# Two attention blocks on one core: pipeline lag 4 to 0, B's PV product in head pairs, and warmup transposes in the tail

## The chip, the cores and the metric

The kernel runs on one core of one Trainium2 chip. The metric is the device time of one execution in microseconds (us). Times quoted are medians. A ratio is the mean time of one kernel's fast runs over the mean of the fast runs of the kernel before from the same rounds, so it is not quite the ratio of the medians beside it.

Engines are named as the profile names them: PE is TensorE (PEld its weight loads), ACT is ScalarE, DVE is VectorE, SP issues the transfers.

## The reference

There are two attention blocks, A and B, over cached keys and values, concatenated at the end. B has its own K and V for each of 32 heads; in A, 8 query heads share one of 4 K/V heads. Everything is bf16, and x is 16 batches of 32 query rows.

```python
# A: Hkv = 4 (repeated 8 times), B: 32 K/V heads; Sk = 1024, Dh = 128, D = 1024
q = (x @ wq).reshape(B, Sq, H, Dh).transpose(0, 2, 1, 3)
scores = einsum("bhqd,bhkd->bhqk", q, k) * Dh ** -0.5
o = einsum("bhqk,bhkd->bhqd", softmax(scores), v)
out = o.transpose(0, 2, 1, 3).reshape(B, Sq, H * Dh) @ wo
# result: concatenate([A's out, B's out], axis=-1)
```

## The kernel before

The work is cut into 128 units of B and 128 of A. A unit is four heads of one batch, so 4 x 32 = 128 query rows. One loop iteration takes one unit of B and one of A through scores, maximum, exponential, transpose of the probabilities, PV, norm and transpose of the output. It also transposes the keys of the next unit and does about one projection group of 8 matmuls. A ran four iterations behind B. This is the loop, cut:

```python
A_LAG = 4
for i in range(-1, last_it + 1):          # last_it = NU + A_LAG + 2, NU = 128
    ia = i - A_LAG
    sc("B", i)                            # scores: 8 matmuls, 32 weight columns x 512
    ot_evac("A", ia - 2, "act")           # ACT: A's transposed output to SBUF
    maxop("B", i)                         # DVE
    pv("B", i - 1)
    norm("B", i - 1)                      # DVE
    sc("A", ia); maxop("A", ia)
    expop("B", i)                         # ACT
    kt_B(i + 1, 0); kt_B(i + 1, 1)        # 16 transposes of keys, copied out by ACT
    proj(i, 0)                            # a projection group: 8 matmuls x 512
    recip("B", i); expop("A", ia)
    kt_B(i + 1, 2); kt_B(i + 1, 3)
    ...
    ot("B", i - 1); ot_evac("B", i - 1, "dve")
    pt("B", i); pt_evac("B", i)           # 8 transposes of the probabilities
    if (ia + 1) % 2 == 0:
        kt_A((ia + 1) // 2)               # every second iteration: A's keys
    pv("A", ia - 1); recip("A", ia); norm("A", ia - 1)
    ...
    pt("A", ia); pt_evac("A", ia)
    ot("A", ia - 1)                       # 1 transpose, reads what norm wrote
    # then the loads of the next units on SP
```

And this is B's PV. Each head has 32 query rows, so its weights (the transposed probabilities) fill only 32 of the array's 128 columns. Four heads sit beside each other, each with its own V:

```python
for c in range(KC):                       # 8 chunks of 128 keys
    for hh in range(4):
        e.matmul(PS[32*hh:32*hh+32, O_BANK, 0:DH], PTs[P][:, c, 32*hh:32*hh+32],
                 VB[u % NVB][:, hh, c, :], start=(c == 0), stop=(c == KC - 1),
                 tile_position=(0, 32 * hh))
```

## Time and profile before

| | before |
|---|---|
| time, median | 991.3 us (4 runs, 990.7 to 993.0) |
| PE busy | 926 of 991 us |
| first scores of B; second; last | 25.4; 33.0; 949.6 us |
| iteration, mean of numbers 5 to 119 | 7.23 us |
| iteration with / without A's key transposes (median) | 7.49 / 6.97 us |
| after the last scores of B | 41.4 us |

An iteration is read from the timeline as the distance between two starts of B's scores. Every second iteration also transposes A's keys. Those are the ones called "even" in the prediction (they are the odd-numbered ones in the code); the ones without are called "odd" there. I write "with keys" and "without keys" below. (The prediction's 7.53 and 7.01 us are single iterations; the medians are a little shorter.)

From the page of the kernel before: span, busy times, transfers, the chain that ended last by engine, and the group of B's PV.

```profile
span 991.0 us, 34534 instructions
PE 926.1 (93%) x15168; PEld 648.7 (65%) x15168; DVE 629.5 (64%) x1456; ACT 656.8 (66%) x1305; POOL 5.2 (1%) x14
DMA packets 172852, 341.96 MB, mean 345 GB/s; under 512 B 7328, under 2 KB 7328, under 8 KB 172704
PE 81%; DVE 8%; ACT 7%; issue 3%; DMA 1%; SPq 0%; POOL 0%; DVEq 0%; ACTq 0%
...
L576 PE MATMUL PS<-VB,PT_B 128*32 128x128 bf16 x4096 | 80.6, 220 | 0.4 <-ACT QO_A L626 0.4
```

PE carries 81% of the chain. The page's busy time cannot say how long PV occupies PE, because its matmuls overlap: 4096 matmuls of 220 ns each would be 901 us, and the union shows 80.6. The distance from one group's first start to the next group's first start says it. These are lines of the timeline of the kernel before (start us, length us, engine, line, operation, tiles, count, idle time before it).

```profile
506.97 0.62 PE L493 MATMUL PS<-KTB,QO_B 128*32 128x512 bf16 x8
507.50 0.48 PEld L576 LDWEIGHTS PS<-VB,PT_B 128*32 128x32 bf16 x32 [0.41 <-issue]
507.53 0.63 PE L576 MATMUL PS<-VB,PT_B 128*32 128x128 bf16 x32
507.92 0.18 PEld L493 LDWEIGHTS PS<-KTA,QO_A 128*32 128x32 bf16 x8
507.97 0.62 PE L493 MATMUL PS<-KTA,QO_A 128*32 128x512 bf16 x8
508.52 0.90 PEld L452 LDWEIGHTS PS<-ident,KB 128*128 128x128 bf16 x16 [0.42 <-issue]
```

PV starts at 507.53 and A's scores at 507.97: PV holds PE for 0.44 us. It streams 32 x 128 = 4096 columns in that time. One stream moves 128 columns in about 56 ns (16 key transposes in 0.90 us), so four must run side by side. The weights of A's scores are loaded ahead: their first load (507.92) precedes their first matmul.

Two waits of PE recur. In an iteration with keys, PE waits for ACT to empty a bank before A's key transposes; in every iteration it waits for DVE's norm before A's output transpose. Same kernel, timeline:

```profile
504.56 1.09 ACT L456 COPY KTB<-PS 128x512 uint32<-128x512 uint32 x2
504.57 0.61 PE L552 MATMUL PS<-ident,P_B 128*128 128x128 bf16 x8
505.31 0.61 PE L468 MATMUL PS<-ident,KA 128*128 128x128 bf16 x8
506.20 0.61 PE L552 MATMUL PS<-ident,P_A 128*128 128x128 bf16 x8
506.40 0.35 DVE L601 TENSOR_SCALAR O_A<-PS,rinv_A 128x128 bf16<-128x128 f32 x1 [0.42 <-PE PS L588]
506.81 0.23 PE L612 MATMUL PS<-ident,O_A 128*128 128x128 bf16 x1
```

Eight transposes take 0.45 us from start to start where nothing waits. The key transposes begin 0.74 us after the group before them (0.29 us waiting), and the output transpose 0.61 us after its predecessor (0.16 us; 0.33 us in the next iteration, without keys).

### The profile page before, as it was taken

What the parts mean: (1) busy time and instruction counts of PE and PEld (TensorE: products, weight loads), DVE (VectorE), ACT (ScalarE), POOL (GpSimd) and SP (SyncE); (2) the same over time, 40 slices, a digit from 0 to 9 for tenths busy, and PEclk for the clock granted to TensorE, in tenths of its full rate; (3) what the DMA queues carried; (4) which work ended last, traced back from release to release, by engine and by line L of the source; (5) the groups of instructions that cost most, each with busy time, mean ns of one, the idle gap of its engine ahead of it and who ended that gap; (6) DMA issues with size and microseconds to landing.
All of it is one profiled execution on the core that took longest, in us unless ns stands there. A gap on an engine that the chain in (4) does not pass through costs nothing.

```text
span 991.0 us, 34534 instructions
## 1 busy us (share of the span) xinstructions
PE 926.1 (93%) x15168; PEld 648.7 (65%) x15168; DVE 629.5 (64%) x1456; ACT 656.8 (66%) x1305; POOL 5.2 (1%) x14
## 2 busy tenths in 40 slices
PE   6899899899999999999999999999999999989985
PEld 3566667666676666667666666766666676666652
DVE  0346666666566666666677666776667777776762
ACT  2667677676676767777666776667676666766641
POOL 0000000000000000000000000000000000000000
PEclk9999999999999999999999999999999999999996
DMA  9998999999999999999999999999999999999800
GB/s 339 387 347 291 388 386 342 329 386 386 378 363 372 366 370 343 386 344 386 361 356 373 355 381 343 383 361 363 372 345 385 343 388 358 369 389 339 302 26 21
DMA packets 172852, 341.96 MB, mean 345 GB/s; under 512 B 7328, under 2 KB 7328, under 8 KB 172704
## 3 DMA queue, kind: packets, MB, share of 16 engines
q1 hardware_dynamic: 172064, 337.67, 94.0%
q8 instruction: 119, 1.95, 0.8%
q0 software_dynamic: 640, 2.10, 0.5%
q14 instruction: 29, 0.24, 0.1%
HBM read 337.64 MB, written 2.10 MB: 343 GB/s over the span
## 4 chain that ended last, share of the span: by engine, by line
PE 81%; DVE 8%; ACT 7%; issue 3%; DMA 1%; SPq 0%; POOL 0%; DVEq 0%; ACTq 0%
PE PS L452 22%; PE PS L493 12%; PE PS L368 11%; PE PS L345 11%; PE PS L552 8%; PE PS L576 6%; DVE PT_B L562 4%; PE PS L468 4%; PE PS L612 3%; PE PS L588 3%; ACT KTB L456 2%; ACT P_B L524 2%; DVE O_A L601 2%; ACT P_A L524 1%; DMA W_Q<-in_B_wq_dram 1%
## 5 line engine op out<-in xcount | busy, mean ns | idle before, releaser
L452 PEld LDWEIGHTS PS<-ident,KB 128*128 128x128 bf16 x4096 | 238.4, 98 | 98.4 <-issue 52.2
L452 PE MATMUL PS<-ident,KB 128*128 128x128 bf16 x4096 | 272.8, 219 | 14.8 <-ACT KTB L456 14.5
L456 ACT COPY KTB<-PS 128x512 uint32<-128x512 uint32 x512 | 275.3, 599 | 1.0 <-PE PS L452 0.9
L524 ACT ACTIVATE P_B<-PS,nmx_B 128x1024 bf16<-128x1024 f32 x128 | 142.5, 1113 | 199.3 <-DVE P_B L513 199.3
L513 DVE TENSOR_SCALAR_CACHE_REDUCE P_B<-PS 128x1024 bf16<-128x1024 f32 x128 | 156.7, 1224 | 55.6 <-PE PS L493 49.7
L513 DVE TENSOR_SCALAR_CACHE_REDUCE P_A<-PS 128x1024 bf16<-128x1024 f32 x128 | 155.5, 1215 | 2.8 <-PE PS L493 2.7
L524 ACT ACTIVATE P_A<-PS,nmx_A 128x1024 bf16<-128x1024 f32 x128 | 145.4, 1136 | 10.2 <-DVE P_A L513 10.2
L629 DVE COPY QO_B<-PS 128x128 bf16<-128x128 bf16 x128 | 28.7, 224 | 164.4 <-PE PS L612 164.4
L562 DVE COPY PT_B<-PS 128x512 uint32<-128x512 uint32 x128 | 88.5, 692 | 31.7 <-PE PS L552 31.7
L562 DVE COPY PT_A<-PS 128x512 uint32<-128x512 uint32 x128 | 88.5, 692 | 12.3 <-PE PS L552 6.5
L576 PEld LDWEIGHTS PS<-VB,PT_B 128*32 128x32 bf16 x4096 | 62.4, 96 | 46.6 <-issue 45.5
L626 ACT COPY QO_A<-PS 128x128 bf16<-128x128 bf16 x128 | 34.0, 265 | 74.4 <-PE PS L612 74.4
L493 PE MATMUL PS<-KTA,QO_A 128*32 128x512 bf16 x1024 | 79.6, 381 | 2.1 <-DVE PT_A L562 2.1
L552 PE MATMUL PS<-ident,P_A 128*128 128x128 bf16 x1024 | 78.5, 220 | 2.8 <-ACT P_A L524 2.8
L576 PE MATMUL PS<-VB,PT_B 128*32 128x128 bf16 x4096 | 80.6, 220 | 0.4 <-ACT QO_A L626 0.4
L588 PE MATMUL PS<-VA,PT_A 128*128 128x128 bf16 x1024 | 79.1, 220 | 1.9 <-DVE QO_B L629 1.2
L493 PE MATMUL PS<-KTB,QO_B 128*32 128x512 bf16 x1024 | 78.8, 384 | 0.7 <-ACT KTB L456 0.7
L552 PE MATMUL PS<-ident,P_B 128*128 128x128 bf16 x1024 | 78.1, 219 | 0.7 <-ACT P_B L524 0.7
L552 PEld LDWEIGHTS PS<-ident,P_A 128*128 128x128 bf16 x1024 | 62.9, 98 | 4.3 <-ACT P_A L524 3.3
L345 PE MATMUL PS<-xT_B,W_Q 128*128 128x512 bf16 x256 | 62.8, 392 | 2.6 <-DMA W_Q<-in_B_wq_dram 2.6
L588 PEld LDWEIGHTS PS<-VA,PT_A 128*128 128x128 bf16 x1024 | 60.4, 98 | 5.7 <-DVE QO_B L629 1.4
L552 PEld LDWEIGHTS PS<-ident,P_B 128*128 128x128 bf16 x1024 | 62.5, 98 | 0.9 <-ACT P_B L524 0.9
(50 smaller groups left out, 817.6 us busy)
## 6 DMA issues: line engine op xcount, KB each, us to landing
KB<-in_B_k_cache_dram SPq DMA_DIRECT2D x128, 1024.0 KB, 7.6
VB<-in_B_v_cache_dram SPq DMA_DIRECT2D x128, 1024.0 KB, 8.5
KA<-in_A_k_cache_dram SPq DMA_DIRECT2D x64, 256.0 KB, 7.8
VA<-in_A_v_cache_dram SPq DMA_DIRECT2D x64, 256.0 KB, 7.9
W_Q<-in_B_wq_dram SPq DMA_DIRECT2D x16, 512.0 KB, 8.9
W_O<-in_B_wo_dram SPq DMA_DIRECT2D x16, 512.0 KB, 8.5
W_Q<-in_A_wq_dram SPq DMA_DIRECT2D x12, 512.0 KB, 9.1
W_O<-in_A_wo_dram SPq DMA_DIRECT2D x8, 512.0 KB, 8.3
```

What stands on the lines that cost most here:

```text
L345: last = e.matmul(PS[:, pbank, 0:T], W[slot][:, c, j * DH:(j + 1) * DH], xT[P][:, c, :], start=(c == 0), stop=(c == DC - 1))
L368: last = e.matmul(PS[:, pbank, :], QO[P][s][:, j, 4 * tg:4 * tg + 4, :].rearrange("p b q -> p (b q)"), W[slot][:, j, nh * 512:(nh + 1) * 5 ...
L452: last = e.transpose(psbf(bk)[:, c * 128:(c + 1) * 128], KB[u % NKB][:, hh, c, :], ident[:])
L456: plan.use("act", lambda e: e.copy(KTB[hs][:].bitcast(U32), PS[:, bk, :].bitcast(U32)), writes=[r_KTB[hs]], banks=[bank[bk]], name="ktev_B ...
L468: last = e.transpose(psbf(bk)[:, c * 128:(c + 1) * 128], KA[m % NKA][:, c, :], ident[:])
L493: last = e.matmul(PS[32 * hh:32 * hh + 32, sbk + half, :], QO[P][s][:, 4 * jh + hh, b, :], kts[hh][:, half * 512:(half + 1) * 512], start= ...
L513: plan.use("dve", lambda e: e.tensor_scalar(Psb[P][:], PS[:, sbk:sbk + 2, :], -scale, None, ALU.mult, ALU.min, accum_out=nmx[P][:, k:k + 1 ...
L524: plan.use("act", lambda e: e.activation(Psb[P][:], PS[:, sbk:sbk + 2, :], AF.Exp, bias=nmx[P][:, k:k + 1], scale=scale, accum_out=rsum[P] ...
L552: last = e.transpose(psbf(bk)[:, c * 128:(c + 1) * 128], src, ident[:])
L562: plan.use("dve", lambda e: e.tensor_copy(PTs[P][:].rearrange("p c n -> p (c n)").bitcast(U32), PS[:, bk, :].bitcast(U32)), writes=[r_PT[P ...
L576: last = e.matmul(PS[32 * hh:32 * hh + 32, O_BANK, 0:DH], PTs[P][:, c, 32 * hh:32 * hh + 32], VB[u % NVB][:, hh, c, :], start=(c == 0), st ...
L588: last = e.matmul(PS[:, O_BANK, 0:DH], PTs[P][:, c, :], VA[m % NVA][:, c, :], start=(c == 0), stop=(c == KC - 1))
```

## The change

It has three parts. The lag goes from 4 to 0, to shorten the ends of the pipeline. B's PV takes heads in pairs: 16 matmuls of 64 weight columns by 256 moving columns replace 32 of 32 by 128; half of each result (a head's probabilities with the other head's V) is thrown away. And 28 transposes of the identity matrix are put into each of the last iterations, to keep PE's clock up. The core of the diff, cut:

```diff
-A_LAG = 4
+A_LAG = 0
+WARM = 28
+PV_PAIRS = True
...
+            if P == "B" and PV_PAIRS:
+                    for c in range(KC):
+                        for pr in range(2):
+                            last = e.matmul(PS[64 * pr:64 * pr + 64, O_BANK, 0:2 * DH],
+                                            PTs[P][:, c, 64 * pr:64 * pr + 64],
+                                            VB[u % NVB][:, 2 * pr:2 * pr + 2, c, :],
+                                            start=(c == 0), stop=(c == KC - 1), tile_position=(0, 64 * pr))
...   # norm over 256 columns, two output transposes, two copies of half the width
+                    e.transpose(PS[:, O_BANK, 256:320].bitcast(BF16), Osb[P][:, 0:DH], ident[:])
+                    return e.transpose(PS[:, O_BANK, 320:384].bitcast(BF16), Osb[P][:, DH:2 * DH], ident[:])
...
+            if A_LAG == 0:       # A's x transposes and 4 projections move ahead of the loop
+                prologue_jobs += [("xT", "A", c0) for c0 in range(0, DC, CPB)]
+                prologue_jobs += q_groups("A", 0, "O", range(4))
...
             flush("dve")
+            if i >= NU and WARM:
+                warm(WARM)
             pt("A", ia)
```

More of the change, by code (lines that the diff above doesn't have):

```diff
@@ L206, in build_kernel @@
         PTs = {P: sb("PT_" + P, [128, KC, 128], BF16) for P in "AB"}
-        Osb = {P: sb("O_" + P, [128, 128], BF16) for P in "AB"}
+        Osb = {P: sb("O_" + P, [128, 256 if (P == "B" and PV_PAIRS) else 128], BF16) for P in "AB"}
         outsb = [sb("outsb%d" % i, [128, N], BF16) for i in range(2)]
@@ L261, in valid, with rs @@
             return 0 <= u < NU
+        def rs(P, u):
+            if P == "A" and u >= NU - A_LAG and (u - (NU - A_LAG)) % 2 == 1 and NU > 2 * A_LAG:
+                return "B"
+            return P
         plan.use("pool", lambda e: e.memset(ones[:], 1.0), writes=[r_ones], name="ones")
@@ L480, in sc @@
             s = g % 2
-            sbk = S_BANK[P]
+            sbk = S_BANK[rs(P, u)]
             if P == "B":
@@ L510, in maxop @@
                 return
-            sbk = S_BANK[P]
+            R = rs(P, u)
+            sbk = S_BANK[R]
             k = u % 4
-            plan.use("dve", lambda e: e.tensor_scalar(Psb[P][:], PS[:, sbk:sbk + 2, :], -scale, None,
+            plan.use("dve", lambda e: e.tensor_scalar(Psb[R][:], PS[:, sbk:sbk + 2, :], -scale, None,
                                                       ALU.mult, ALU.min, accum_out=nmx[P][:, k:k + 1]),
-                     writes=[r_P[P], r_nmx[P][k]], banks=[bank[sbk], bank[sbk + 1]], name="max_%s_%d" % (P, u))
+                     writes=[r_P[R], r_nmx[P][k]], banks=[bank[sbk], bank[sbk + 1]], name="max_%s_%d" % (P, u))
             expect(bank[sbk], ("S", P, u))
@@ L521, in expop @@
                 return
-            sbk = S_BANK[P]
+            R = rs(P, u)
+            sbk = S_BANK[R]
             k = u % 4
-            plan.use("act", lambda e: e.activation(Psb[P][:], PS[:, sbk:sbk + 2, :], AF.Exp,
+            plan.use("act", lambda e: e.activation(Psb[R][:], PS[:, sbk:sbk + 2, :], AF.Exp,
                                                    bias=nmx[P][:, k:k + 1], scale=scale,
                                                    accum_out=rsum[P][:, k:k + 1]),
-                     reads=[r_nmx[P][k]], writes=[r_P[P], r_rsum[P][k]], banks=[bank[sbk], bank[sbk + 1]],
+                     reads=[r_nmx[P][k]], writes=[r_P[R], r_rsum[P][k]], banks=[bank[sbk], bank[sbk + 1]],
                      name="exp_%s_%d" % (P, u))
@@ L531, in expop @@
             r_rsum[P][k].tag = u
-            r_P[P].tag = u
+            r_P[R].tag = (P, u)
         def recip(P, u):
@@ L545, in pt @@
                 return
-            bk = S_BANK[P]
+            R = rs(P, u)
+            bk = S_BANK[R]
             def fn(e):
@@ L550, in fn @@
                 for c in range(KC):
-                    src = Psb[P][:, c // 4, (c % 4) * 128:(c % 4 + 1) * 128]
+                    src = Psb[R][:, c // 4, (c % 4) * 128:(c % 4 + 1) * 128]
                     last = e.transpose(psbf(bk)[:, c * 128:(c + 1) * 128], src, ident[:])
                 return last
-            expect(r_P[P], u)
-            plan.use("pe", fn, reads=[r_P[P], r_ident], banks=[bank[bk]], name="pt_%s_%d" % (P, u))
+            expect(r_P[R], (P, u))
+            plan.use("pe", fn, reads=[r_P[R], r_ident], banks=[bank[bk]], name="pt_%s_%d" % (P, u))
             bank[bk].tag = ("PT", P, u)
@@ L560, in pt_evac @@
                 return
-            bk = S_BANK[P]
+            bk = S_BANK[rs(P, u)]
             plan.use("dve", lambda e: e.tensor_copy(PTs[P][:].rearrange("p c n -> p (c n)").bitcast(U32),
@@ L570, in pv, with fn @@
                 return
-            if P == "B":
+            if P == "B" and PV_PAIRS:
+                def fn(e):
+                    last = None
+                    for c in range(KC):
[4 more added lines that the diff above has]
+                                            start=(c == 0), stop=(c == KC - 1), tile_position=(0, 64 * pr))
+                    return last
+                rd = [r_VB[u % NVB]]
+            elif P == "B":
                 def fn(e):
@@ L600, in norm @@
             k = u % 4
-            plan.use("dve", lambda e: e.tensor_scalar(Osb[P][:], PS[:, O_BANK, 0:DH], rinv[P][:, k:k + 1], None,
+            w = 2 * DH if (P == "B" and PV_PAIRS) else DH
+            plan.use("dve", lambda e: e.tensor_scalar(Osb[P][:], PS[:, O_BANK, 0:w], rinv[P][:, k:k + 1], None,
                                                       ALU.mult),
@@ L611, in ot, with fn, warm @@
             expect(r_O[P], u)
-            plan.use("pe", lambda e: e.transpose(PS[:, O_BANK, 128:192].bitcast(BF16), Osb[P][:], ident[:]),
-                     reads=[r_O[P], r_ident], banks=[bank[O_BANK]], name="ot_%s_%d" % (P, u))
-            bank[O_BANK].tag = ("OT", P, u)
+            if P == "B" and PV_PAIRS:
+                def fn(e):
+                    e.transpose(PS[:, O_BANK, 256:320].bitcast(BF16), Osb[P][:, 0:DH], ident[:])
+                    return e.transpose(PS[:, O_BANK, 320:384].bitcast(BF16), Osb[P][:, DH:2 * DH], ident[:])
+                plan.use("pe", fn, reads=[r_O[P], r_ident], banks=[bank[O_BANK]], name="ot_%s_%d" % (P, u))
+            else:
+                plan.use("pe", lambda e: e.transpose(PS[:, O_BANK, 128:192].bitcast(BF16), Osb[P][:], ident[:]),
+                         reads=[r_O[P], r_ident], banks=[bank[O_BANK]], name="ot_%s_%d" % (P, u))
+            bank[O_BANK].tag = ("OT", P, u)
+        def warm(n):
+            bk = next_kt_bank()
+            def fn(e):
+                last = None
+                for c in range(n):
+                    last = e.transpose(psbf(bk)[:, (c % 8) * 128:(c % 8 + 1) * 128], ident[:], ident[:])
+                return last
+            plan.use("pe", fn, reads=[r_ident], banks=[bank[bk]], name="warm_%d" % len(plan.streams["pe"].ops))
+            bank[bk].tag = ("warm",)
         def ot_evac(P, u, eng):
@@ L620, in ot_evac @@
             s = g % 2
+            expect(bank[O_BANK], ("OT", P, u))
+            r_QO[P][s][b][jh].tag = ("OT", g)
+            if P == "B" and PV_PAIRS:
+                R = PS[:, O_BANK, 256:384].bitcast(BF16)
+                for hl in range(2):
+                    src = R.rearrange("p (a x) -> p a x", x=SQ)[:, 5 * hl:5 * hl + 3:2, :]
+                    dst = QO[P][s][:, 4 * jh + hl:4 * jh + 4:2, b, :]
+                    if eng == "act":
+                        fn = (lambda e, dst=dst, src=src: e.copy(dst, src))
+                    else:
+                        fn = (lambda e, dst=dst, src=src: e.tensor_copy(dst, src))
+                    plan.use(eng, fn, writes=[r_QO[P][s][b][jh]], banks=[bank[O_BANK]],
+                             name="otev_%s_%d%s" % (P, u, "ab"[hl]))
+                return
             dst = QO[P][s][:, 4 * jh:4 * jh + 4, b, :]
             src = PS[:, O_BANK, 128:192].bitcast(BF16).rearrange("p (j q) -> p j q", q=SQ)
-            expect(bank[O_BANK], ("OT", P, u))
-            r_QO[P][s][b][jh].tag = ("OT", g)
             if eng == "act":
@@ L674, in build_kernel @@
         if FAST:
-            assert A_LAG >= 4
             prologue_jobs += [("xT", "B", c0) for c0 in range(0, DC, CPB)]
             prologue_jobs += q_groups("B", 0, "Q", range(4))
-            for c0 in range(0, DC, CPB):
-                put(("xT", "A", c0), 0)
-            for j in range(8):
-                put(("q", "A", 0, j, "O"), 1 + j // 2)
-            rb0 = min(5, NB - 5)
+            if A_LAG == 0:
+                prologue_jobs += [("xT", "A", c0) for c0 in range(0, DC, CPB)]
+                prologue_jobs += q_groups("A", 0, "O", range(4))
+                for j in range(4, 8):
+                    put(("q", "A", 0, j, "O"), 0)
+                a_done = 0
+            else:
+                for c0 in range(0, DC, CPB):
+                    put(("xT", "A", c0), 0)
+                for j in range(4):
+                    put(("q", "A", 0, j, "O"), min(A_LAG - 1, (j * A_LAG) // 4))
+                for j in range(4, 8):
+                    put(("q", "A", 0, j, "O"), min(A_LAG, A_LAG - 1 + (j - 3) // 2))
+                a_done = A_LAG
+            rb0 = min(a_done + 1, NB - 5)
             for k_, j in enumerate(range(4, 8)):
@@ L685, in build_kernel @@
             slot_free["Q"] = rb0 + 3
-            slot_free["O"] = 4
+            slot_free["O"] = a_done
         else:
```

## The prediction

> **What bounds it now.** TensorE. The page has PE busy 926 of 991 us, and the chain of waits lies 81% on PE. The view of waits shows almost nothing in which PE waits for data in the steady part: its only DMA waits are 6.3 and 2.6 us at the start. DMA is nearly full too (0.99 busy in the steady stretch), but its queue waits for buffers that PE frees (420 us for K, 229 us for V). One loop iteration takes 7.26 us (123 of them between 56.3 and 949.6 us); in the timeline even and odd ones take 7.53 and 7.01 us.
>
> **B's PV in pairs** decides the case. Today 32 matmuls of 32 weight columns by 128 moving columns run four at a time: the timeline has the next PE group 0.44 to 0.47 us after PV's start, which is 4096 columns on four concurrent streams (4096/4/2.4 per ns = 0.43 us; 128-column transposes start every 56 ns). Paired, 16 matmuls stream 256 columns each on two concurrent streams, and half of the result is thrown away: 16 x 256/2 = 2048 columns in sequence, about 0.86 us. So fewer instructions, but +0.43 us of PE per iteration. Added besides: a second output transpose (+0.06 us PE), norm over 256 instead of 128 columns (0.35 to about 0.48 us DVE), two output copies for one (0.22 to about 0.32 us DVE), and a change between 64- and 32-column tiles. The Trainium skill, page "TensorEngine Tiling (Array Packing)", section Key Properties, says that changing tiling mode drains TensorE; this trace has about 0.1 us extra between the four-column scores and 128-wide work. I allow 0 to 0.1 us.
>
> How much is exposed: in odd iterations PE has only a 0.33 us gap before A's output transpose, which follows from the transposes before it and shifts along: +0.5 us. In even iterations PE waits 0.29 us for ScalarE's K evacuation before A's K transposes; that wait absorbs half: +0.25 us. The few iterations without a projection wait about 1.1 us for ScalarE and absorb nearly all. Mean about +0.4 us over some 118 iterations: **+48 us**. DVE (64% busy) takes its +0.23 us off the path.
>
> **Lag 4 to 0.** PE's work is the same; only idle time at the ends can go. Four A-only iterations at the tail (about 5 us each, half idle, 951 to 978 us) vanish; the head gets A's x transposes and four more projections (9 us) before the first scores, and a first iteration of about 12 us. Summed up: -3 us (0 to -8).
>
> **Warmup.** 28 transposes in three tail iterations, in gaps. The last projections now run at half clock (8 matmuls 3.6 us instead of 1.9). The skill's page "TensorE: Matmul & The Clock Gate", Part 4, doubts that transposes keep the clock up; 32 transposes from 6.3 us here didn't raise it before 18 us. Worth -3 to +2 us; about 0.
>
> **Prediction:** 1036 us, range 1016 to 1055. Faster by over 2%: 0.02; within 2%: 0.10; slower by over 2%: 0.88.
>
> **What would show it.** Right: the PV group of B has 2048 matmuls and the next PE group starts about 0.87 us after it; steady iterations near 7.65 us, odd ones grow more than even ones; the wait of A's K transposes for ScalarE shrinks; mean DMA rate falls; after the last B score the tail is about 13 us shorter and the head as much longer. Wrong: iterations stay at 7.26 us, or PV still takes 0.45 us.
>
> **What would make it wrong.** If pairs of 64 columns don't run concurrently, PV takes 1.7 us and the time goes above 1130. If more of the extra 0.43 us hides in waits that I count as shifting along, or the ends give back more than 8 us, the result is nearer 1010.

## The result, and the profile after

The changed kernel takes 1041.9 us (8 runs, 1040.9 to 1043.2), against 991.1 us (13 runs) for the kernel before. The ratio is 1.0509, with a 95% interval of 1.0498 to 1.0519. It is 5% slower.

| | before | after |
|---|---|---|
| first scores of B; second; last | 25.4; 33.0; 949.6 us | 34.5; 48.2; 1014.5 us |
| iteration, mean of numbers 5 to 119 | 7.23 us | 7.65 us |
| with / without keys | 7.49 / 6.97 us | 7.83 / 7.63 us |
| PV of B, start to next group (median) | 0.44 us | 0.99 us |
| after the last scores of B | 41.4 us | 25.6 us |

The page of the changed kernel, the same lines:

```profile
span 1040.1 us, 30991 instructions
PE 1003.3 (96%) x13332; PEld 698.4 (67%) x13332; DVE 672.6 (65%) x1584; ACT 668.9 (64%) x1305; POOL 5.2 (0%) x14
DMA packets 172839, 341.73 MB, mean 329 GB/s; under 512 B 7328, under 2 KB 7328, under 8 KB 172704
PE 87%; ACT 5%; DVE 3%; issue 3%; DMA 1%; SPq 0%; POOL 0%; ACTq 0%; DVEq 0%
...
L586 PE MATMUL PS<-VB,PT_B 128*64 128x256 bf16 x2048 | 136.2, 276 | 0.4 <-ACT QO_A L677 0.4
```

There are 1836 fewer matmuls and PE is busy 77 us longer. PV's union grew from 80.6 to 136.2 us with half the matmuls. The transfers are the same bytes at a lower rate. That they are not the cause is shown by fill_kt2 below, which moves as much (341.97 MB) in 950 us. The timeline of the changed kernel, around one PV and before A's key transposes:

```profile
535.86 0.61 PE L500 MATMUL PS<-KTB,QO_B 128*32 128x512 bf16 x8
536.40 0.80 PEld L586 LDWEIGHTS PS<-VB,PT_B 128*64 128x64 bf16 x16 [0.42 <-issue]
536.40 1.06 PE L586 MATMUL PS<-VB,PT_B 128*64 128x256 bf16 x16
537.39 0.12 PEld L500 LDWEIGHTS PS<-KTA,QO_A 128*32 128x32 bf16 x8 [0.20 <-issue]
537.39 0.61 PE L500 MATMUL PS<-KTA,QO_A 128*32 128x512 bf16 x8
...
541.58 0.61 PE L562 MATMUL PS<-ident,P_B 128*128 128x128 bf16 x8
542.02 0.61 PE L475 MATMUL PS<-ident,KA 128*128 128x128 bf16 x8
```

PV now holds PE from 536.40 to 537.39, 0.99 us. The weights of A's scores are no longer loaded ahead: PEld is idle 0.20 us, and the load and the first matmul start together. The last two lines show where part of the cost vanished: A's key transposes follow 0.44 us after the group before them, so the 0.29 us of waiting for ACT is gone.

### The profile page after: what moved, and what is told of

The parts are those of the page before. It is cut to its first block, busy times and chain, and to the rows that moved or that the text cites. A ratio compares the mean times of both kernels' runs of the same rounds, so it can differ in the third digit from the quotient of the medians.

```text
span 1040.1 us, 30991 instructions
## 1 busy us (share of the span) xinstructions
PE 1003.3 (96%) x13332; PEld 698.4 (67%) x13332; DVE 672.6 (65%) x1584; ACT 668.9 (64%) x1305; POOL 5.2 (0%) x14
## 4 chain that ended last, share of the span: by engine, by line
PE 87%; ACT 5%; DVE 3%; issue 3%; DMA 1%; SPq 0%; POOL 0%; ACTq 0%; DVEq 0%
PE PS L459 21%; PE PS L500 13%; PE PS L352 11%; PE PS L375 11%; PE PS L586 11%; PE PS L562 8%; PE PS L609 7%; PE PS L475 3%; PE PS L640 3%; DVE QO_B L670 2%; ACT P_B L533 2%; ACT KTB L463 2%; ACT P_A L533 1%; DMA W_Q<-in_B_wq_dram 1%; PE PS L637 1%
## 5 line engine op out<-in xcount | busy, mean ns | idle before, releaser
L670 DVE COPY QO_B<-PS 128x64 bf16<-128x64 bf16 x256 | 49.0, 192 | 204.0 <-PE PS L637 199.7
L586 PEld LDWEIGHTS PS<-VB,PT_B 128*64 128x64 bf16 x2048 | 101.9, 109 | 54.5 <-issue 54.5
L586 PE MATMUL PS<-VB,PT_B 128*64 128x256 bf16 x2048 | 136.2, 276 | 0.4 <-ACT QO_A L677 0.4
L609 PEld LDWEIGHTS PS<-VA,PT_A 128*128 128x128 bf16 x1024 | 60.0, 98 | 15.9 <-DVE QO_B L670 15.6
```

The costliest lines, as they stand in the source:

```text
L586: last = e.matmul(PS[64 * pr:64 * pr + 64, O_BANK, 0:2 * DH], PTs[P][:, c, 64 * pr:64 * pr + 64], VB[u % NVB][:, 2 * pr:2 * pr + 2, c, :], ...
L609: last = e.matmul(PS[:, O_BANK, 0:DH], PTs[P][:, c, :], VA[m % NVA][:, c, :], start=(c == 0), stop=(c == KC - 1))
L670: fn = (lambda e, dst=dst, src=src: e.tensor_copy(dst, src))
```

## The experiments

My theory: the pairs double the columns that PE streams in sequence, which costs 0.43 us for each unit; the change of tile width and the second transpose add to it; waits absorb a part; the lag only moves idle time at the ends. Rivals: the missing lag couples A and B and is part of the loss; the 64-column tiles themselves are slow; the wider norm and the doubled copies on DVE are the cause.

### One part at a time

lag_only and after_nowarm set constants of the changed kernel; lag_warm too. pairs_only has lag 4 with the projections placed as in the kernel before.

```diff
 lag_only:      +WARM = 0      +PV_PAIRS = False
 lag_warm:                     +PV_PAIRS = False
 after_nowarm:  +WARM = 0
 pairs_only:    +A_LAG = 4     +WARM = 0
```

> The changed kernel with the pairs and the warmup taken out: only the lag goes from 4 to 0. My theory (the lag moves only idle time at the two ends): about 989 us, 1 to 4 us under the kernel before; iterations stay at 7.26 us; the stretch after the last B scores about 14 us shorter than the 41.4 us of before, the stretch before the second B scores longer by about as much. Rival (the missing lag couples A and B more tightly and is itself part of the loss): 1000 us or more, iterations over 7.4 us.

> Lag 0 and the 28 warmup transposes, no pairs. If transposes keep TensorE's clock up in the tail: 3 to 5 us under lag_only, the last projections (groups of 8 matmuls) at 1.9 us each. If transposes do not count as activity: equal to lag_only within 1 us, with last groups of 3 us or more in both.

> The changed kernel without the warmup transposes. If the warmup works: 2 to 5 us slower than the changed kernel (ratio to before about 1.054 to 1.056 against 1.051) with slow projections at the end. If it does nothing: ratio 1.051.

> The kernel before with the paired PV alone (lag 4, no warmup). If the pairs cause all of the loss and the parts simply add: about 1042 us, that is 51 us over before (126 iterations times 0.41 us), iterations near 7.67 us. If lag 0 is part of the loss: clearly less, 1010 to 1030 us.

All four ran, with 991.4 us for the kernel before, and all are correct.

| | time, median | ratio to before (95%) | mean iteration |
|---|---|---|---|
| pairs_only | 1046.0 us | 1.0552 (1.0537 to 1.0566) | 7.68 us |
| after_nowarm | 1040.8 us | 1.0494 (1.0480 to 1.0509) | 7.65 us |
| lag_only | 984.8 us | 0.9931 (0.9918 to 0.9945) | 7.20 us |
| lag_warm | 986.3 us | 0.9942 (0.9929 to 0.9954) | 7.20 us |

The pairs alone cost 1046.0 - 991.4 = 54.7 us, more than the whole loss. The lag gains 6.5 us without the pairs (984.8 against 991.4) and 5.2 us with them (1040.8 against 1046.0). The warmup gains nothing and seems to cost a little: 1.5 us in lag_warm, and 1.1 us in the changed kernel (1041.9 against 1040.8), though both pairs of ratios have overlapping intervals. Do the parts add? Each measured alone, they give 54.7 - 6.5 + 1.5 = 49.7 us, against the 50.5 us between 1041.9 and 991.4: within 1 us. (The chain 54.7 - 5.2 + 1.1 also gives 50.6, but it must, because each step starts where the last one ended.) The rival that blames the missing lag falls: lag_only is faster than the kernel before, and its iterations are not longer.

My expectation for lag_only (989 us) was 4 us too high, and the one for pairs_only (1042 us) 4 us too low. Neither branch of the other two held: lag_warm was not faster than lag_only, yet the last full groups of 8 projections take 1.9 us in both, and after_nowarm was not slower than the changed kernel.

### Columns, tile width, side work

Three kernels at lag 0 with the warmup, to be set against lag_warm and the changed kernel. The three ran (kernel before: 991.7 us), the other two earlier, so the ratios are the better guide. tile32_n256 streams the columns of the pairs through 32-column tiles, with the output layout of the pairs. tile64_n128 uses 64-column tiles for the old number of columns (relative error 0.63, half of the heads get another head's values). Its output is wrong, which doesn't matter for the time. side_only keeps the old PV, but writes it in the layout of the pairs, so that the wide norm, two transposes and two copies stay.

```diff
 tile32_n256, in the changed kernel:
-                        for pr in range(2):
+                        for hh in range(4):
+                            pr = hh // 2          # 32*hh, tile_position (0, 32*hh); VB of both heads of the pair
 tile64_n128, in lag_warm:
-                        for hh in range(4):
+                        for pr in range(2):       # 64*pr, tile_position (0, 64*pr); VB of head 2*pr alone
 side_only, in the changed kernel:
-                            last = e.matmul(PS[64 * pr:64 * pr + 64, O_BANK, 0:2 * DH], ...
+                            last = e.matmul(PS[32*hh:32*hh+32, O_BANK, DH*(hh%2):DH*(hh%2)+DH], ...   # one head's VB
```

> The changed kernel, but its PV in 32 matmuls of 32 weight columns by 256 moving columns, four at a time: the same columns streamed, the same output layout and the same work after it, no change of tile width between scores and PV. Theory of streamed columns: PV still takes about 0.86 us until the next PE group (2048 columns in sequence), time 1028 to 1040 us; what it gains on the changed kernel (0.99 us) is the price of the 64-column tiles. Theory that the 64-column tiles cost the time: PV back near 0.5 us, about 990 to 1000 us. Correct result.

> Lag 0 with warmup, but PV in 16 matmuls of 64 weight columns by only 128 moving columns, and norm, transpose and copy as before the change (wrong result on purpose: half of the heads get another head's values). Theory of streamed columns: PV about 0.43 us plus the price of the tile change, 0.5 to 0.6 us, time 988 to 1003 us. Theory that the 64-column tiles cost the time: PV about 0.9 us, 1025 us or more.

> Lag 0 with warmup, PV as before the change (32 columns by 128) but written into the layout of the pairs, so that the wide norm, the two output transposes and the two copies stay. Theory of streamed columns: only the second transpose (0.06 us) and part of the waits remain, 990 to 1000 us. Theory that the extra VectorE work is the cause: 1015 us or more. Correct result.

| | tile x moving columns | side work of pairs | PV to next group | without keys | with keys | time | ratio to before (95%) |
|---|---|---|---|---|---|---|---|
| lag_warm | 32 x 128 | no | 0.44 us | 6.96 us | 7.49 us | 986.3 us | 0.9942 (0.9929 to 0.9954) |
| side_only | 32 x 128 | yes | 0.44 us | 7.05 us | 7.49 us | 992.3 us | 1.0012 (0.9997 to 1.0028) |
| tile64_n128 | 64 x 128 | no | 0.57 us | 7.12 us | 7.49 us | 993.5 us | 1.0021 (1.0004 to 1.0038) |
| tile32_n256 | 32 x 256 | yes | 0.87 us | 7.48 us | 7.68 us | 1025.8 us | 1.0346 (1.0330 to 1.0361) |
| changed kernel | 64 x 256 | yes | 0.99 us | 7.63 us | 7.83 us | 1041.9 us | 1.0509 (1.0498 to 1.0519) |

Differences here are taken before rounding. PV's own time is a sum: twice the columns add 0.43 us (0.44 to 0.87), the 64-column tile adds 0.12 us at either length. The iterations without keys show every term in full: to 6.96 us come 0.08 (side work), 0.43 (columns) and 0.15 (tile), which makes the 7.63 us. In the iterations with keys, the side work and the tile width alone cost nothing (7.49 in three kernels), and of the whole 0.66 us only 0.35 appear. So 0.32 us is absorbed, about the 0.29 us that PE waited for ACT there. It is also why the tile width costs 7 us at 128 columns but 16 us at 256: in the first case there is a wait left to hide it.

The timeline of tile32_n256 shows the doubled columns without a change of width:

```profile
536.45 1.06 PE L587 MATMUL PS<-VB,PT_B 128*32 128x256 bf16 x32
537.21 0.23 PEld L500 LDWEIGHTS PS<-KTA,QO_A 128*32 128x32 bf16 x8
537.32 0.62 PE L500 MATMUL PS<-KTA,QO_A 128*32 128x512 bf16 x8
```

Here the weights of A's scores are again loaded 0.11 us ahead of their first matmul. The 64-column kernel with short streams lacks that:

```profile
535.45 0.64 PE L597 MATMUL PS<-VB,PT_B 128*64 128x128 bf16 x16
536.02 0.12 PEld L500 LDWEIGHTS PS<-KTA,QO_A 128*32 128x32 bf16 x8
536.02 0.61 PE L500 MATMUL PS<-KTA,QO_A 128*32 128x512 bf16 x8
```

The Trainium skill, page "TensorEngine Tiling (Array Packing)", section Key Properties, says that changing the tiling mode drains TensorE. The traces of tile64_n128 and the changed kernel agree with that: load and first matmul start together after a change of width, and 0.12 us is lost. It is lost at the change and not in the stream. From the first to the last start of PV's matmuls it takes 0.41 us (32 x 128) and 0.42 us (64 x 128), and 0.79 us at 256 columns with either tile. From that last start to A's scores it takes 0.032 and 0.149 us at 128 columns, 0.086 and 0.203 us at 256: 0.117 us more in both (medians over each trace). The way in costs 0.03 us besides: from B's scores to PV it is 0.52 us in lag_warm and tile32_n256, 0.55 us in the two kernels with 64-column tiles. In and out make up the 0.15 us of the sum above.

The theory that 64-column tiles are the main cost falls (1025.8 us with 32-column tiles), and so does the one that blames DVE: side_only costs 6.0 us over lag_warm (7 us by the ratios).

### What the warmup does

In the kernel before, the clock fell in the tail. These are stretches of the tail of the kernel before (from:to us, length, then busy time and count of PE, PEld, DVE, ACT and POOL, the granted clock as a share of full, the busy share of the transfers and their GB/s):

```profile
958.00:960.00 2.00, 1.23 (x17) 0.92 (x17) 0.72 (x3) 1.23 (x3) 0.00 (x0) 1.00 0.00 0
960.00:962.00 2.00, 1.56 (x10) 0.42 (x11) 0.85 (x2) 0.01 (x1) 0.00 (x0) 0.59 0.00 0
962.00:964.00 2.00, 2.00 (x7) 0.70 (x5) 0.77 (x2) 1.20 (x2) 0.00 (x0) 0.55 0.00 0
974.00:978.00 4.00, 2.34 (x18) 1.75 (x18) 1.45 (x4) 0.68 (x3) 0.00 (x0) 0.50 0.00 0
978.00:982.00 4.00, 3.64 (x9) 1.04 (x8) 0.00 (x0) 0.27 (x1) 0.00 (x0) 0.50 0.00 0
982.00:987.00 5.00, 3.67 (x9) 1.04 (x8) 1.13 (x2) 0.00 (x0) 0.00 (x0) 0.50 0.00 0
```

The granted clock is 0.5 to 0.6 of full in five of these. The two groups of 8 projection matmuls in the last two stretches took 3.60 us each there; one in the middle of the kernel takes 1.89. So lag4_warm puts the warmup alone into the kernel before (it runs in seven iterations there). It was made from the changed kernel by its constants, with the projections placed as in the kernel before; this is its difference from the kernel before.

```diff
+            if i >= NU and WARM:          # NU = 128, WARM = 28, A_LAG = 4, no pairs
+                warm(WARM)
```

> The kernel before (lag 4, PV in 32-column tiles) with the 28 warmup transposes alone, in all seven tail iterations. In the kernel before the last projections ran at half clock (8 matmuls 3.1 to 3.6 us, three groups, about 4.6 us lost). If transposes hold the clock: those groups take 1.9 us, and the time is between 2 us under and 4 us over the kernel before (4.6 us won, up to 1.5 us lost for each block on TensorE's path). If transposes do not count: the groups stay at 3 us or more and the time is 2 to 10 us over.

It took 992.4 us (before: 992.1; ratio 1.0002, 0.9987 to 1.0017), and the same stretches read:

```profile
960.00:964.00 4.00, 3.27 (x35) 1.72 (x33) 1.92 (x3) 0.67 (x2) 0.00 (x0) 1.00 0.00 0
974.00:978.00 4.00, 2.98 (x49) 2.55 (x45) 2.22 (x5) 1.47 (x3) 0.00 (x0) 1.00 0.00 0
978.00:982.00 4.00, 3.47 (x43) 2.67 (x44) 0.47 (x2) 0.27 (x1) 0.00 (x0) 1.00 0.01 4
982.00:987.00 5.00, 5.00 (x62) 3.74 (x60) 1.38 (x2) 0.00 (x0) 0.01 (x1) 1.00 0.00 0
```

Transposes do hold the clock: it stays at 1.00 and the last two projections take 1.90 and 1.89 us. The Trainium skill, page "TensorE: Matmul & The Clock Gate", Part 4, says that transposes don't count as PE activity in that way; this run contradicts it. The head of the changed kernel shows that they also raise it: PE begins there with 32 transposes and nothing else; up to 8.7 us they start 107 ns apart, from 8.97 us on 56 ns. (In the kernel before, the same 32 stay at 107 ns to their end at 9.7 us, and the clock rises at 18.3 us.)

The time is nevertheless the same, because each block of 28 holds PE for 1.56 us, and some blocks stand in front of work that was ready. The last projection ends 36.1 us after the last scores of B, against 37.0 us in the kernel before, so 0.9 us is left of the 4.6 us that three faster groups save. One such block, in the timeline of lag4_warm:

```profile
958.24 0.62 PE L607 MATMUL PS<-VA,PT_A 128*128 128x128 bf16 x8 [1.22 <-DVE QO_B L678]
958.70 1.73 PE L648 MATMUL PS<-ident 128*128 128x128 bf16 x28
960.26 0.61 PE L560 MATMUL PS<-ident,P_A 128*128 128x128 bf16 x8
```

In the kernel before, A's transposes of the probabilities started at 959.03, that is 1.10 us after A's PV (957.93); here they start 2.02 us after it. At lag 0 there is nothing to hold: the tail of lag_only, without any warmup, keeps the full clock. This is its last stretch:

```profile
972.00:978.00 6.00, 4.14 (x18) 1.40 (x16) 1.56 (x3) 0.00 (x0) 0.54 (x1) 1.00 0.11 44
```

after_nowarm, the changed kernel without the warmup, keeps it to its last matmul too. So in these traces removing the lag already did what the warmup was for, and in the changed kernel nothing was left for the warmup to gain.

### A version that beats both

The waits pointed to another change. PE waits for DVE's norm before A's output transpose, so fill_kt moves one of the four groups of B's key transposes (of the unit after the next) in front of it. fill_kt_mv also puts A's key transposes behind A's PV. Both start from lag_only.

```diff
 fill_kt:
+            if i == -1:
                 kt_B(i + 1, 0)
             kt_B(i + 1, 1)
...
             pt_evac("A", ia)
+            kt_B(i + 2, 0)
             ot("A", ia - 1)
 fill_kt_mv, besides:
-            if (ia + 1) % 2 == 0: kt_A((ia + 1) // 2)
             pv("A", ia - 1)
+            if (ia + 1) % 2 == 0: kt_A((ia + 1) // 2)
```

> Lag 0, no pairs, no warmup, and one of the four K transposes of B of the next unit but one moved in front of A's output transpose, where TensorE waits for VectorE's norm (0.3 us in odd iterations). Theory that this wait is on the path: odd iterations 6.96 to about 6.65 us, even ones about 0.15 us less, time 955 to 968 us. If the transfers are the next limit, not under about 945 us. If the wait merely moves: 980 us or more.

> The same with A's K transposes moved behind A's PV, so that in even iterations TensorE does not wait 0.3 us for ScalarE's K copies. Theory: even iterations another 0.2 to 0.3 us shorter than in fill_kt, 940 to 955 us, unless the transfers (340 MB, 0.99 busy) hold it at about 945 to 950 us, which would show as TensorE waiting for DMA landings.

Both missed: 985.3 us (ratio 0.9928, 0.9913 to 0.9943) and 986.8 us (0.9950, 0.9933 to 0.9966), no better than lag_only. The waits show why. First the leading wait of PE on VectorE in lag_only, then the leading wait of fill_kt:

```profile
PE PS L640 <- DVE O_A L623: 10.6, 63, 0.4
```

```profile
PE PS L597 <- ACT QO_A L677: 42.2, 126, 0.4
```

The wait for DVE has gone, and a new one of 0.33 us stands in 126 iterations: B's PV waits until ACT has copied A's transposed output out of the bank. In ACT's queue the copy of the early keys stood in front of that copy, and the trace has them in this order: keys at 507.96, A's output at 508.45, PV at 508.86 us. fill_kt2 queues A's copy first:

```diff
 fill_kt2, on top of fill_kt:
-            kt_B(i + 2, 0)
+            kt_early = kt_B(i + 2, 0, defer=True)   # transposes now, ACT's copy later
             ot("A", ia - 1)
...  # next iteration
             ot_evac("A", ia - 2, "act")
+            if kt_early is not None:
+                kt_early()                          # ACT's copy of the early keys
```

> fill_kt with ScalarE's order mended: the copy of A's transposed output is queued ahead of the copy of the early K transposes, so that B's PV no longer waits 0.33 us for it. Theory (in fill_kt the wait had only moved there): odd iterations 7.06 to about 6.73 us, even ones 7.46 to about 7.13 us, time 942 to 955 us. If the transfers are the real limit behind it (340 MB at the 387 GB/s that the head of the trace shows is 6.9 us for an iteration), the time stops at 950 to 970 us and TensorE shows waits for landings. If it stays at 984, my reading of the waits is wrong.

It took 950.3 us (before: 992.0; ratio 0.9583, 0.9570 to 0.9596), correct: 4.2% faster than the kernel before and nearly 9% faster than the changed one. The timelines, fill_kt first, from B's scores to its PV:

```profile
507.91 0.61 PE L500 MATMUL PS<-KTB,QO_B 128*32 128x512 bf16 x8
508.86 0.63 PE L597 MATMUL PS<-VB,PT_B 128*32 128x128 bf16 x32 [0.33 <-ACT QO_A L677]
```

```profile
505.61 0.62 PE L505 MATMUL PS<-KTB,QO_B 128*32 128x512 bf16 x8
506.12 0.63 PE L602 MATMUL PS<-VB,PT_B 128*32 128x128 bf16 x32
```

PV now starts 0.51 us after the scores, not 0.95. The mean iteration fell from 7.20 us (lag_only and fill_kt) to 6.93 us; without keys it is 6.63, with keys 7.28 us. Those with keys still wait about 0.25 us for ACT, and gained less than I expected (7.13 us). The waits of PE in this kernel show no landing of a transfer after the start. But by one measure little room is left: from 60 to 900 us its transfers run at 378 GB/s (364 in the kernel before), and the expectation took the 387 GB/s of the head as their limit, or 6.9 us for an iteration. How much further this goes, and whether fill_kt_mv's move would help now, was not tried.

## Why the prediction was right

The direction, the cause and the size held: 1036 us was predicted with a range of 1016 to 1055, and 1041.9 us was measured.

- **PV in pairs.** The term for the streamed columns, +0.43 us, was exact (tile32_n256 against 32 x 128). PV itself took 0.99 us rather than the 0.87 us that I named as the sign. The missing 0.12 us is the change of tile width, which I left out of the sign. For the whole change, in and out, I allowed 0 to 0.1 us; it costs 0.15 us.
- **What is exposed.** I said +0.5 us without keys and +0.25 us with keys; it was +0.66 and +0.35 (against lag_warm). The ordering and the reason (the wait for ACT absorbs) held: 0.32 us absorbed, 0.29 us of wait measured before. Iterations without a projection hid nearly all, as said: one at 928.6 us took 6.55 us before, one at 1007.9 us 6.63 us after. That the mean came out at the 7.65 us that I named is partly luck: both usual kinds grew by more than I said, and the 15 of 115 iterations without a projection grew by less than 0.1 us.
- **A sign that misled.** I said that the wait of A's key transposes for ACT would shrink. In the timeline it vanished (0.74 to 0.44 us between starts). The view of waits doesn't show it: it has 3.7 us before and 4.2 us after, in 8 and 9 places. It counts idle time after modelled ends of matmuls, and the pipeline's tail of the group before covers a wait of 0.29 us.
- **The lag.** Predicted -3 us (0 to -8), measured -6.5 us alone and -5.2 us with the pairs. The ends moved as described (the tail 15.9 us shorter, the second scores of B 15.2 us later). In lag_only they nearly cancel (18.3 us shorter, 15.8 us later), and the stretch between the second and last scores is 6.2 us shorter, because work of A now stands in the head. That it gained more than 3 us is likely because the shorter tail keeps the clock up, which I had counted under the warmup: the kernel before lost some 4.6 us to slow groups there. That split was not measured by itself.
- **The warmup.** Predicted about 0, measured +1.1 to +1.5 us. The doubt whether transposes hold the clock was unfounded: the sign I took from the head of the kernel before is not repeated in the head of the changed one, where transposes alone raised it. At lag 0 the clock just didn't need it.
- **VectorE.** Its extra work was said to be off the path. side_only bounds all side work together at 6.0 us, of which the second transpose (0.06 us for each unit) is a part.

The pairs were missized by about 7 us (48 against 54.7), the lag by about 2 the other way, the warmup by 1. So a part of the closeness is errors that cancel.

## What to carry to other kernels

On PE count the columns that stream in sequence, not the instructions: here half as many, wider matmuls with half of the result discarded cost their columns, 0.43 us for each unit. A gap in which PE waits for another engine absorbs new PE work only in the iterations that have it, so cost a change for each kind of iteration. And when a wait is filled with other work, look at the order in the queue of every engine which that work uses: fill_kt gained nothing until ScalarE's queue was put in order, and then 34 us.

## What the Trainium skill lacked or had wrong

- "TensorE: Matmul & The Clock Gate", Part 4, says that transposes don't engage the full clock. In lag4_warm blocks of 28 transposes held the granted clock at 1.00 through a tail where it had been 0.50, and they ran at 56 ns each (28 in 1.56 us). In the head of the changed kernel transposes alone raised it (107 ns apart, then 56 ns from 8.97 us on).
- The same page, in "Back-to-back issue gap", gives about 81 ns for a matmul of 128 columns and 131 ns for one of 512 where each has its own weight load. Here 16 transposes with a weight load each took 0.90 us (56 ns each), and 8 projection matmuls of 512 columns with a weight load each 1.73 us (216 ns each). These are the 56 and 216 ns that the section gives for an isolated matmul.
- "TensorEngine Tiling (Array Packing)", Key Properties, says that a change of tiling mode drains the engine but gives no price. Going from 32 to 64 columns and back cost 0.15 us here: 0.03 on the way in (0.52 to 0.55 us from B's scores to PV) and 0.12 on the way out (PV from 0.44 to 0.57, and from 0.87 to 0.99 us).
- "TensorE: Matmul & The Clock Gate", Part 1, ties the fall of the clock to an idle window of about 3.4 us (further on it says that frequent short idles do it too, without a length or share). In the tail of the kernel before it fell to 0.59 at 960 to 962 us, although PE had been busy 1.23 of the 2 us just before, and none of its idle gaps there was longer than 1.22 us.
